# Copies out of PSUM ahead of sigmoid and weight splits on ScalarE in the dense stage, and a group's last preparation moved behind its output copies

## The chip, the cores and the metric

The kernel runs on one core of a Trainium2 chip. The metric is the device time of one execution in microseconds; lower is better. The engines are TensorE (PE in the profile, its weight loads PEld), VectorE (DVE), ScalarE (ACT), GpSimd (POOL) and SyncE (SP), which only issues transfers here. Each engine runs its own instructions in program order and waits for the others by semaphores.

## The reference, cut to what matters

An attention stage gives 4608 tokens of 512 numbers, a mixture of eight experts follows, and then the dense gated stage in which the change lies:

```python
def _moe2_ref(x, w_gate, w_val, w_out):      # x: 4608 x 512, 1536 hidden columns
    gate = 1.0 / (1.0 + np.exp(-(x @ w_gate)))
    val = x @ w_val
    return (gate * val @ w_out).astype(np.float32)
```

## The kernel before

The first two stages end near 714 us of the profiled execution; the function `ffn` does the dense stage. Every fp32 product is made of three matmuls on operands split into a high part (a rounded copy, made by ScalarE) and a low part (the rest, a subtraction on VectorE).

**Groups and steps.** `ffn` runs over groups `p`. Groups 0 to 3 are wide: 1024 tokens in two halves of 512, multiplied in a scheme of seven products in place of eight (`NK`, `ACTS`). Group 4 is narrow (`single`): 512 tokens in halves of 256. A group has twelve steps `j`, one for each 128 hidden columns. In a step PE makes products 0 to 6 with `prod` (L1417, six matmuls each): product 0 in `begin` of the step before, then `p1` to `p6`, into three kinds of PSUM banks: `ma` (products 0, 3, 4, 6), `mc` (1) and `md` (2, 5). `p5` adds into the `md` bank that `p2` wrote, after ScalarE's copy `v` (L1534) of the first sum; `p4` adds into the `ma` bank after ScalarE's copy `w` (L1539). `p1`'s bank is added to `u` on VectorE (L1523), and ScalarE takes a sigmoid of that (L1524); `p5` ends with an addition on VectorE (L1553) and a second sigmoid (L1554); `p4` with an addition to `v` (L1548); `p6` with the multiply of the gate (L1558), and GpSimd multiplies the other half's gate into `gB[j]` (L1564). Then `down` (L1453, twelve matmuls) adds the step before to the four output banks.

**Weights.** `fetch` reads a step's two weight tiles from memory (SP's queue, L863), `mix` makes sums and differences of them on GpSimd (L872 to L876), and `fill(j, i)` splits slot `i` (L883 on ScalarE, L884 on VectorE): slot 0 serves products 0 and 1, slot 1 products 2 and 3, slot 2 products 4 and 5, slot 3 product 6. `ready` fills slots 1 and 2 of the next step, calls `mix` for the step after it, and in group 0 also splits the output weight with `own(j, 1)`.

**Order.** The program order is written out by hand, and each engine keeps it. In steps 0 to 10 it is p1, p2, p3, p5, p4, `gated`, `ready`, `down(j - 1)`, `begin(j + 1)`, p6; in the last step p2, p3, p1, p4, p5, `gated`, p6, the split of the product, `ready`, `down(j - 1)`. The filling of slot 0 stands at the end of p1, that of slot 3 at the end of p3. After the last step the second half's twelve `down` products follow from `gB`, with transposes for the next group between them (`operands`). `fin` copies the four output banks (ScalarE and VectorE, L1464, L1466) and writes their rows with indirect transfers on GpSimd (L1467); each write waits until the one before has landed. At steps 1 and 2, `load` (L909) reads tokens for the next group, 1 MB each, on SP's queue behind the fetches of the step before.

Of the kernel before, what the change touches and what calls it, by code (L numbers as in the profile page):

```python
# [849 lines left out]
class Group:  # L850
# [60 lines left out]
    def gate(self, m):  # L911
        nc = self.nc
        t = self.tok[m] = self.sp.tile([P, 4], I32, tag="tok", name="tok")
        nc.gpsimd.tensor_copy(t, self.y[m][:, :, DM].bitcast(I32))
        g = self.gt[m] = self.sp.tile([P, 4], F32, tag="gt", name="gt")
        for r in range(4):
            nc.gpsimd.indirect_dma_start(
                out=g[:, r:r + 1], out_offset=None, in_=self.gd,
                in_offset=bass.IndirectOffsetOnAxis(ap=t[:, r:r + 1].bitcast(U32), axis=0))
# [462 lines left out]
def ffn(tc, ctx, c, grp, out):  # L1382
    nc = tc.nc
    V, A = nc.vector, nc.scalar
    NJ = DFF // P
# [9 lines left out]
    def own(j, part):  # L1395
        if part == 0:
            nc.sync.dma_start(out=w2[j][:, 1].bitcast(F32), in_=grp.wd[3 * j + 2])
        else:
            raw = w2[j][:, 1].bitcast(F32)
            A.activation(out=w2[j][:, 0], in_=raw, func=AF.Copy)  # L1400
            V.tensor_tensor(out=w2[j][:, 1], in0=raw, in1=w2[j][:, 0].bitcast(F32), op=ALU.subtract)
# [19 lines left out]
    def fetch(j, kind):  # L1421
        grp.fetch(j, kind, gp.tile([P, 512], F32, tag=("rg", "rv")[kind], name="rw", bufs=1 + kind))
# [3 lines left out]
    def mix(j, part):  # L1426
        if part == 0:
            s12s[j] = grp.dp.tile([P, 512], F32, tag="dsg", name="s12")
            grp.mix(j, s12s[j])
        else:  # L1430
            s34s[j] = gp.tile([P, 512], F32, tag="s34", name="s34", bufs=1)
            grp.mix(j, s12s[j], s34s[j])

    def fill(j, i):
        src = (lambda: grp.raws[j, 0], lambda: s12s[j], lambda: s34s[j], lambda: grp.raws[j, 1][:, 256:512])[i]()
        grp.fill(j, i, grp.slot(i), src)
# [19 lines left out]
    def sums():  # L1456
        return [ps_o.tile([P, DM], F32, tag="o", name="o") for _ in range(4)]

    def fin(m, o):
        tok = grp.tok.pop(m)  # L1460
        for r in range(4):
            t = op.tile([P, DM], F32, tag="os", name="os")
            if r % 2:
                A.activation(out=t, in_=o[r], func=AF.Copy)  # L1464
            else:
                V.tensor_copy(t, o[r])  # L1466
            d = nc.gpsimd.indirect_dma_start(  # L1467
                out=out, out_offset=bass.IndirectOffsetOnAxis(ap=tok[:, r:r + 1].bitcast(U32), axis=0),
                in_=t, in_offset=None)
            if m == NT // 4 - 1:  # L1470
                tc.declare_no_dep(d.ins, group="rows", reason="each token is in one place of the packed order")
                tc.add_to_no_dep_group("rows", d.ins)
# [4 lines left out]
    def begin(p, j):  # L1477
        a = bank("ma")
        prod(a, j, 0, True, False)
        u = gp.tile([P, 512], F32, tag="u", name="u")  # L1480
        A.activation(out=u[:, 0:grp.n], in_=a[:, 0:grp.n], func=AF.Copy)  # L1481
        banks[p, j] = a, u

    for p in range(NP + 1):
        single = p == NP
        n = 256 if single else 512
        if p == 0:
            fetch(1, 0)
            fetch(1, 1)
            mix(1, 0)  # L1490
            mix(1, 1)
            for j in range(NJ):
                own(j, 0)
            begin(p, 0)
        gB = []
        if not single:
            for tag in ("k3", "k4", "k5"):
                t = grp.kx.tile([P, 4, 512], F32, tag=tag, name="gb")
                gB += [t[:, i] for i in range(4)]
        o = sums()  # L1500
        g = None
        for j in range(NJ):
            end = j == NJ - 1
            one, two = (not single or j < NJ - k for k in (1, 2))
            n1, n2 = (j + 1) % NJ, (j + 2) % NJ
            a, sg = banks.pop((p, j))
            if j > 0:
                split(st["sg"], slice(0, 512), g)()
            if not single and p < NP:
                nxt = [2 * p + 2] + ([2 * p + 3] if p + 1 < NP else [])  # L1510
                for i, m in enumerate(nxt):
                    if j == 1 + i:
                        grp.load(m)
                    if j == 4 + i:
                        grp.gate(m)
                    if j == 7 + i:
                        grp.mult(m)
            now = {}

            def p1():  # L1520
                now["c"] = cb = bank("mc")
                prod(cb, j, 1, True, True)
                V.tensor_tensor(out=sg[:, 0:n], in0=sg[:, 0:n], in1=cb[:, 0:n], op=ALU.add)  # L1523
                A.activation(out=sg[:, 0:n], in_=sg[:, 0:n], func=AF.Sigmoid)  # L1524
                if one:
                    fill(n1, 0)
                if two:
                    fetch(n2, 0)

            def p2():  # L1530
                now["d"] = db = bank("md")
                prod(db, j, 2, True, False)
                now["v"] = t = gp.tile([P, 512], F32, tag="v", name="v", bufs=1)
                A.activation(out=t[:, 0:n], in_=db[:, 0:n], func=AF.Copy)  # L1534

            def p3():
                prod(a, j, 3, False, False)
                now["w"] = u = gp.tile([P, 512], F32, tag="w", name="w", bufs=1)
                A.activation(out=u[:, 0:n], in_=a[:, 0:n], func=AF.Copy)  # L1539
                if j > 0:  # L1540
                    fill(j, 3)
                if two:
                    fetch(n2, 1)

            def p4():
                t = now["v"]
                prod(a, j, 4, False, False)
                V.tensor_tensor(out=t[:, 0:n], in0=t[:, 0:n], in1=a[:, 0:n], op=ALU.add)  # L1548

            def p5():  # L1550
                db, u = now["d"], now["w"]
                prod(db, j, 5, False, True)
                V.tensor_tensor(out=u[:, 0:n], in0=u[:, 0:n], in1=db[:, 0:n], op=ALU.add)  # L1553
                A.activation(out=sg[:, n:] if single else u, in_=u[:, 0:n], func=AF.Sigmoid)  # L1554

            def p6():
                prod(a, j, 6, False, True)
                V.tensor_tensor(out=sg[:, 0:n], in0=sg[:, 0:n], in1=a[:, 0:n], op=ALU.mult)  # L1558

            def gated():  # L1560
                if single:
                    V.tensor_tensor(out=sg[:, n:], in0=sg[:, n:], in1=now["v"][:, 0:n], op=ALU.mult)
                else:
                    nc.gpsimd.tensor_tensor(out=gB[j], in0=now["w"], in1=now["v"], op=ALU.mult)  # L1564

            def ready():
                if p == 0:
                    own(j, 1)
                if one:
                    fill(n1, 1)  # L1570
                    fill(n1, 2)
                if two:
                    mix(n2, 0)
                    mix(n2, 1)

            for f in (p2, p3, p1, p4, p5) if end else (p1, p2, p3, p5, p4):
                f()
            gated()
            if end:
                p6()  # L1580
                last, g = g, pieces()
                split(sg, slice(0, 512), g)()
                ready()
                down(o, j - 1, last)
            else:
                ready()
                if j > 0:
                    down(o, j - 1, g)
                begin(p, j + 1)
                p6()  # L1590
                g = pieces()
            st["sg"] = sg
        if single:
            down(o, NJ - 1, g)
            return lambda: fin(2 * p, o)
        steps = grp.operands(p + 1, bank, small)
        h = pieces()
        split(gB[0], slice(0, 512), h)()
        next(steps)
        next(steps)  # L1600
        down(o, NJ - 1, g)
        fin(2 * p, o)
        fill(0, 3)
        o = sums()
        g = h
        for j in range(NJ):
            if j + 1 < NJ:
                h = pieces()
                split(gB[j + 1], slice(0, 512), h)()
            if j in (1, 2, 4, 5, 7, 8):  # L1610
                next(steps)
            down(o, j, g)
            g = h
        for _ in steps:
            pass
        begin(p + 1, 0)
        fin(2 * p + 1, o)
# [64 lines left out]
```

## Time and profile before

| | us |
|---|---|
| median of 3 runs | 1617.02 (1615.57 to 1620.66) |
| the profiled execution | 1617.71 |
| its span, first to last instruction | 1616.0 |
| PE busy | 1489.8 (92%) |
| PE waiting for the copy `v` (L1534) at `md` products | 38.7, in 51 waits |

A row of the timeline gives the start in us from the span's start, how long the row lasts, engine, line, operation, written tile <- read tiles, shape and count; in brackets the engine's idle time before it and what ended it. Neighbouring instructions of one kind are merged in one row (x6: six matmuls). Matmuls overlap, so the distance of two starts says more than a row's length.

### The profile page before, as it was taken

To read this page: it belongs to the slowest core of one execution; us is meant where nothing else is said; L and a number is where in the kernel's file an instruction comes from. 1 tells how busy PE (TensorE), PEld (TensorE's weight loads), DVE (VectorE), ACT (ScalarE), POOL (GpSimd) and SP (SyncE) were. 2 spreads that over 40 slices of the span, in tenths; PEclk is the share of its full clock that TensorE was granted. 3 is DMA by queue.
4 is the path that set the end of the run, shared out by engine and by line. 5 is a ranking of instruction groups with operands and counts; after the bars stand their busy time and mean duration, and the time that the engine had idled before them with its cause. 6 is when DMAs were issued, how large, how long until landed. Compare 5 with 4: busy or idle time off the path is not lost.

```text
span 1616.0 us, 22768 instructions
## 1 busy us (share of the span) xinstructions
PE 1489.8 (92%) x7314; PEld 1224.2 (76%) x7314; DVE 891.0 (55%) x1547; ACT 695.4 (43%) x1250; POOL 701.4 (43%) x688
## 2 busy tenths in 40 slices
PE   6889589999999998999999899999999999999887
PEld 3778468877888876877777777777777777778776
DVE  7788745444454544355556455565555645555554
ACT  3456444355333333354444434444344434443443
POOL 5554044344544556424663146532565234532322
PEclk7889889999999999999999999999999999999999
DMA  9874354475444463223111111112111121110211
GB/s 251 235 209 154 131 183 130 143 201 177 152 131 151 160 222 110 73 100 116 40 40 52 66 66 41 50 41 86 59 40 40 40 79 40 47 45 27 79 61 45
DMA packets 110407, 165.96 MB, mean 103 GB/s; under 512 B 23207, under 2 KB 68263, under 8 KB 108080
## 3 DMA queue, kind: packets, MB, share of 16 engines
q1 hardware_dynamic: 97904, 124.84, 25.6%
q0 software_dynamic: 10112, 28.88, 5.4%
q10 hardware_dynamic: 2240, 10.50, 1.8%
q8 instruction: 60, 0.98, 0.3%
q14 instruction: 91, 0.75, 0.1%
HBM read 126.41 MB, written 38.31 MB: 102 GB/s over the span
## 4 chain that ended last, share of the span: by engine, by line
PE 38%; ACT 6%; DVE 6%; issue 5%; DMA 2%; POOL 0%; POOLq 0%; ACTq 0%; DVEq 0%
PE o L1453 17%; PE ma L1417 14%; PE md L1417 6%; ACT wu L883 2%; ACT gh L1440 2%; DVE u L1523 2%; DVE u L1558 2%; DMA out<-os,tok 2%; ACT v L1534 1%; DVE wu L884 0%; PE b L942 0%; PE y L1084 0%; PE h L1084 0%; PE mc L1417 0%; PE a L942 0%
## 5 line engine op out<-in xcount | busy, mean ns | idle before, releaser
L1453 PE MATMUL o<-w,gh 128*128 128x512 f32 x864 | 270.2, 394 | 2.3 <-ACT os L1464 2.3
L1417 PE MATMUL md<-x,wu 128*128 128x512 f32 (+1 forms) x720 | 176.5, 381 | 38.7 <-ACT v L1534 38.7
L1453 PEld LDWEIGHTS o<-w,gh 128*128 128x128 f32 x864 | 160.7, 189 | 36.9 <-ACT os L1464 4.0
L1417 PEld LDWEIGHTS md<-x,wu 128*128 128x128 f32 x720 | 125.2, 191 | 79.0 <-ACT v L1534 58.4
L1564 POOL TENSOR_TENSOR gb<-w,v 128x512 f32<-128x512 f32 x48 | 75.0, 1563 | 242.2 <-DVE v L1548 179.8
L1417 PE MATMUL ma<-xT,wu 128*128 128x512 f32 (+1 forms) x720 | 170.0, 372 | 2.8 <-DVE v L1548 2.6
L1417 PE MATMUL ma<-x,wu 128*128 128x512 f32 (+1 forms) x720 | 167.5, 368 | 2.1 <-DVE x L948 2.1
L1453 PE MATMUL o<-w,gl 128*128 128x512 f32 x432 | 168.9, 391 | 0.0
L1417 PEld LDWEIGHTS ma<-xT,wu 128*128 128x128 f32 x720 | 128.2, 190 | 28.0 <-issue 4.2
L1417 PEld LDWEIGHTS ma<-x,wu 128*128 128x128 f32 x720 | 127.7, 188 | 25.6 <-DVE x L948 2.4
L884 DVE TENSOR_TENSOR wu<-rw,wu 128x256 fp32r<-128x256 f32 (+1 forms) x118 | 73.2, 621 | 107.8 <-ACT wu L883 107.8
L1084 PE MATMUL h<-h,xh 128*128 128x512 f32 x304 | 125.0, 411 | 7.6 <-ACT xh L1072 6.8
L884 DVE TENSOR_TENSOR wu<-s,wu 128x512 fp32r<-128x512 f32 x120 | 123.0, 1065 | 0.1
L1084 PE MATMUL h<-l,xh 128*128 128x512 f32 x304 | 121.8, 401 | 0.0
L1084 PE MATMUL h<-h,xl 128*128 128x512 f32 x304 | 121.8, 401 | 0.0
L1467 POOL DMA_INDIRECT out<-os,tok x36 | 37.4, 1039 | 187.8 <-DVE os L1466 107.4
L1481 ACT ACTIVATE u<-ma 128x512 f32<-128x512 f32 (+1 forms) x60 | 33.3, 556 | 169.3 <-PE ma L1417 165.9
L1558 DVE TENSOR_TENSOR u<-u,ma 128x512 f32<-128x512 f32 (+1 forms) x60 | 38.0, 634 | 119.0 <-PE ma L1417 119.0
L1148 POOL TENSOR_TENSOR dl<-dl,dsg 128x512 f32<-128x512 f32 x36 | 46.2, 1283 | 129.8 <-DVEq L1204 103.4
L1073 DVE TENSOR_TENSOR xl<-T,xh 128x512 fp32r<-128x512 f32 x38 | 26.3, 692 | 131.7 <-ACT xh L1072 130.5
L872 POOL TENSOR_TENSOR s<-rw 128x256 f32<-128x256 f32 x59 | 62.2, 1054 | 78.9 <-DMA rw<-wd 38.1
L1453 PEld LDWEIGHTS o<-w,gl 128*128 128x128 f32 x432 | 81.5, 189 | 17.4
(293 smaller groups left out, 3211.8 us busy)
## 6 DMA issues: line engine op xcount, KB each, us to landing
rw<-wd SPq DMA_DIRECT2D x118, 256.0 KB, 2.8
raw<-moe_w SPq DMA_DIRECT2D x46, 512.0 KB, 6.1
wd<-dw SPq DMA_DIRECT2D x36, 256.0 KB, 2.0
q<-q SPq DMA_DIRECT2D x8, 1024.0 KB, 6.6
k<-k SPq DMA_DIRECT2D x8, 1024.0 KB, 8.7
vb<-v SPq DMA_DIRECT2D x64, 128.0 KB, 4.8
xd<-xs ACTq DMA_DIRECT2D x8, 1024.0 KB, 4.5
draw<-moe_w_gate SPq DMA_DIRECT2D x12, 512.0 KB, 4.1
```

What stands on the lines that cost most here:

```text
L872: G.tensor_tensor(out=s12[:, lo], in0=v[:, lo], in1=v[:, hi], op=ALU.add)
L883: self.nc.scalar.activation(out=t[:, 0], in_=src, func=AF.Copy)
L884: self.nc.vector.tensor_tensor(out=t[:, 1], in0=src, in1=t[:, 0].bitcast(F32), op=ALU.subtract)
L1084: nc.tensor.matmul(ps, lhsT=a, rhs=b, start=(first and k == 0), stop=(last and k == n - 1))
L1148: G.tensor_tensor(out=lf, in0=lf, in1=s.bitcast(F32), op=ALU.mult)
L1417: nc.tensor.matmul(ps[:, 0:n], lhsT=w[:, a, cc * P:(cc + 1) * P], rhs=x[cc][:, b, 0:n], start=(first and i == 0), stop=(last and i == 5), ...
L1440: A.activation(out=gh[:, at], in_=src, func=AF.Copy)
L1453: nc.tensor.matmul(o[r], lhsT=a, rhs=b, start=(j == 0 and k == 0), stop=(j == NJ - 1 and k == 2))
L1467: d = nc.gpsimd.indirect_dma_start(out=out, out_offset=bass.IndirectOffsetOnAxis(ap=tok[:, r:r + 1].bitcast(U32), axis=0), in_=t, in_offse ...
L1481: A.activation(out=u[:, 0:grp.n], in_=a[:, 0:grp.n], func=AF.Copy)
L1558: V.tensor_tensor(out=sg[:, 0:n], in0=sg[:, 0:n], in1=a[:, 0:n], op=ALU.mult)
L1564: nc.gpsimd.tensor_tensor(out=gB[j], in0=now["w"], in1=now["v"], op=ALU.mult)
```

## The change

ScalarE's copies `v` and `w` keep their places behind p2 and p3. The sigmoid behind p1, with the filling of slot 0 and the first fetch, becomes a function `gate` that is called after p3 (in the last step after p4). The filling of slot 3 and the second fetch leave p3 and become `rest`, called after p4 (in the last step after p5, directly ahead of p6). In the last step `ready` is called after `fin(2 * p, o)` and not ahead of `down(j - 1)`; and `own(11, 1)` of group 0, which belonged to it, is made in step 10.

```diff
@@ p1
                 V.tensor_tensor(out=sg[:, 0:n], in0=sg[:, 0:n], in1=cb[:, 0:n], op=ALU.add)
+
+            def gate():
                 A.activation(out=sg[:, 0:n], in_=sg[:, 0:n], func=AF.Sigmoid)
                 if one:
                     fill(n1, 0)
@@ p3
                 A.activation(out=u[:, 0:n], in_=a[:, 0:n], func=AF.Copy)
+
+            def rest():
                 if j > 0:
                     fill(j, 3)
                 if two:
@@ ready
-                if p == 0:
+                if p == 0 and not end:
                     own(j, 1)
+                    if j == NJ - 2:
+                        own(j + 1, 1)
                 if one:
                     fill(n1, 1)
                     fill(n1, 2)
...
-            for f in (p2, p3, p1, p4, p5) if end else (p1, p2, p3, p5, p4):
+            for f in (p2, p3, p1, p4, gate, p5, rest) if end else (p1, p2, p3, gate, p5, p4, rest):
                 f()
             gated()
             if end:
                 p6()
                 last, g = g, pieces()
                 split(sg, slice(0, 512), g)()
-                ready()
                 down(o, j - 1, last)
...
         fin(2 * p, o)
+        ready()
         fill(0, 3)
```

## Rows read from the trace of the kernel before

**Rows 1.** The page: span, and busy time, share and instructions of each engine.

```profile
span 1616.0 us, 22768 instructions
PE 1489.8 (92%) x7314; PEld 1224.2 (76%) x7314; DVE 891.0 (55%) x1547; ACT 695.4 (43%) x1250; POOL 701.4 (43%) x688
```

**Rows 2.** PE's waits, groups 0 to 4 in turn: total us, times, longest us.

```profile
PE md L1417 <- ACT v L1534: 4.6, 10, 1.2
...
PE md L1417 <- ACT v L1534: 7.6, 10, 4.4
...
PE md L1417 <- ACT v L1534: 5.3, 10, 2.1
...
PE md L1417 <- ACT v L1534: 6.6, 10, 3.4
...
PE md L1417 <- ACT v L1534: 14.5, 11, 1.9
```

**Rows 3.** Timeline of PE, middle step of group 1: p2, p3, p5, p4.

```profile
940.63 1.52 PE L1417 MATMUL md<-x,wu 128*128 128x512 f32 x6
941.99 1.52 PE L1417 MATMUL ma<-x,wu 128*128 128x512 f32 x6
943.87 1.66 PE L1417 MATMUL md<-x,wu 128*128 128x512 f32 x6 [0.35 <-ACT v L1534]
945.37 1.52 PE L1417 MATMUL ma<-xT,wu 128*128 128x512 f32 x6
```

**Rows 4.** Timeline of ScalarE, same step: p1's sigmoid and the copy `v`.

```profile
942.18 0.63 ACT L1524 ACTIVATE u<-u 128x512 f32<-128x512 f32 x1 [1.36 <-DVE u L1523]
...
943.24 0.58 ACT L1534 ACTIVATE v<-md 128x512 f32<-128x512 f32 x1
```

**Rows 5.** Timeline of VectorE, same step: slots 1 and 2, then the multiply.

```profile
947.54 2.39 DVE L884 TENSOR_TENSOR wu<-s,wu 128x512 fp32r<-128x512 f32 x2
952.37 0.69 DVE L1558 TENSOR_TENSOR u<-u,ma 128x512 f32<-128x512 f32 x1 [2.43 <-PE ma L1417]
```

**Rows 6.** Timeline of PE, narrow group: p2, p3, p5 of step 10; p1, p4 of 11.

```profile
1588.83 0.88 PE L1417 MATMUL md<-x,wu 128*128 128x256 f32 x6
1589.55 0.88 PE L1417 MATMUL ma<-x,wu 128*128 128x256 f32 x6
1591.75 0.98 PE L1417 MATMUL md<-x,wu 128*128 128x256 f32 x6 [1.32 <-ACT v L1534]
...
1598.90 0.88 PE L1417 MATMUL mc<-x,wu 128*128 128x256 f32 x6
1599.88 0.98 PE L1417 MATMUL ma<-xT,wu 128*128 128x256 f32 x6
```

**Rows 7.** Timeline of group 1's last step: the copy for slot 3, p5, p6.

```profile
1058.84 0.41 ACT L883 ACTIVATE wu<-rw 128x256 fp32r<-128x256 f32 x1
...
1060.81 1.52 PE L1417 MATMUL md<-x,wu 128*128 128x512 f32 x6
...
1062.99 1.60 PE L1417 MATMUL ma<-xT,wu 128*128 128x512 f32 x6 [0.66 <-DVE v L1548]
```

**Rows 8.** Timeline of GpSimd and SP at group 1's start: output writes and a load.

```profile
915.42 0.96 POOL L1467 DMA_INDIRECT out<-os,tok  x1 [2.52 <-DMA out<-os,tok]
915.52 0.42 SPq L909 DMA_DIRECT2D yt<-yd  x1
...
925.67 0.96 POOL L1467 DMA_INDIRECT out<-os,tok  x1 [9.28 <-DMA out<-os,tok]
```

**Rows 9.** Stretches after two waits: length, busy us of engines, PEclk, DMA share, GB/s.

```profile
926.90:933.70 6.80, 5.09 (x12) 4.08 (x13) 1.69 (x2) 2.54 (x5) 3.99 (x5) 0.50 0.33 114
...
1317.00:1324.00 7.00, 3.58 (x16) 2.63 (x15) 2.39 (x4) 2.37 (x6) 5.74 (x6) 1.00 0.11 42
```

**Rows 10.** Timeline of SP and GpSimd, narrow group: fetches, and the first `mix` operation.

```profile
1582.86 0.87 SPq L863 DMA_DIRECT2D rw<-wd  x2
...
1586.20 0.73 POOL L872 TENSOR_TENSOR s<-rw 128x256 f32<-128x256 f32 x1 [6.29 <-DMA rw<-wd]
```

## The prediction, made before the changed kernel ran

> **What bounds the kernel now.** I read the page first: the span is 1616.0 us and nothing but TensorE is near full [rows 1]. The change touches the dense stage alone (`ffn`, from about 714 us on), so I then asked for the waits of PE in five stretches, one for each group: four wide ones (512 tokens twice, twelve steps each, then the second sum) and the narrow last one (256). In all five one wait leads, PE at an `md` product for ScalarE's copy `v` (L1534) [rows 2]. Then the timeline of one middle step, engine by engine, says why. PE issues p1, p2, p3 without a gap, each 1.36 us after the last, but p5 starts 1.88 us after p3 and p4 1.50 us after p5 [rows 3]. p5 adds into the bank that `v` is copied from, so it needs that copy. ScalarE is in order and has p1's sigmoid, at 942.18, and the copy of fill(n1,0) in front of it; `v` starts at 943.24 and ends at 943.82, PE starts at 943.87 [rows 3, 4]. p2's last matmul had ended at 942.15 (940.63 + 1.52). So the wait is one of queue order: `v` could have run a microsecond sooner. A middle step loses 0.52 + 0.14 = 0.66 us, of which the waits view shows 0.35; the other 0.31 is the restart. In the narrow group a product takes 0.72 us and p5 comes 2.20 us after p3: 1.48 lost, 1.32 of it in the view [rows 6].
>
> **Term A, p5 in the wide groups.** The change moves `v` and `w` in front of the sigmoid. `v` can start about 0.1 after p2's end, at 942.25, and end at 942.83; p5 could start at 943.35. Covered by 0.5. `w` starts after p3 (941.99 + 1.52 = 943.51), ends near 944.20, and p4 would start at 944.71: covered by 0.5 as well. What is moved behind: the sigmoid and fill(n1,0) now run near 944.2 to 945.4 instead of 942.2 to 943.3. Queued behind them are u's sigmoid, fill(j,3), fill(n1,1) and fill(n1,2), and on VectorE their subtractions. `begin` of the next step needs fill(n1,0) at about 948.8 (after p4 and twelve matmuls); the subtraction ends near 946, cover over 2 us. fill(j,3), behind u's sigmoid in the changed order, ends near 948.2; p6 needs it at about 950.2, cover 2 us. The last subtractions (2.39 us for two) ended at 949.93 and the next multiply on VectorE started at 952.37 [rows 5]; they move to about 950.6 and the multiply to 951.7, cover 1.1 us. Where a cover is gone, PE pays the excess in every step. On SP's queue fetch(n2,1) goes behind fill(j,3), some 3 us later, and GpSimd's mix with it; the result is wanted one step later. So the whole loss goes. From the four wide rows: 4.6 + 7.6 + 5.3 + 6.6 = 24.1 us in 40 waits [rows 2]; less the longest of the last three (4.4, 2.1, 3.4 = 9.9, term D), 14.2 in 37 waits, plus 37 x 0.31 of restarts: 25.7. Bounds: 25.7, or 19.8 if p4 has to wait 0.16 for `w` in each of 37 steps (the narrow group's last step shows such a wait: p4 starts at 1599.88 with `w` directly ahead of it, 0.98 after p1, which a row puts at 0.72 for a product [rows 6]; less 0.1 for the longer cover). I take 25.4.
>
> **Term B, the narrow group.** 14.5 in 11 waits, plus 11 x 0.16: 16.3 [rows 2, 6]. Here the covers are thin: `v` would end some 0.05 ahead of p5, and `w` likewise ahead of p4, since a product lasts 0.72 only. I leave 0.25 a step. In step 0 there is no down product to cover fill(1,0), which is now 2 us later, and the first steps also wait for mix(2) behind the output writes on GpSimd: 1.6 more. fetch(n2,1) is the other queue: the two fetches were issued from 1582.86 and mix started at 1586.20 [rows 10]; 2.5 us later still leaves mix a microsecond ahead of its reader. 16.3 - 2.7 - 1.6 = 12; bounds 9 and 16. PE idled for up to 1.9 here; if a fall of the clock as in [rows 9] goes with these waits, up to 3.4 more comes back, of which I add 0.9.
>
> **Term C, the end steps pay.** In a group's last step p6 follows p5 directly. Before, fill(j,3) was done early (1058.84, 0.41 us) and p6 waited for VectorE's add to `v` only: it started 2.18 after p5 instead of 1.36 [rows 7]. Now that add runs sooner, but fill(j,3) stands behind u's sigmoid, and that behind p5 itself. p5 ends at 1062.33; add u to about 1063.1, sigmoid (0.63 [rows 4]) to 1063.8, copy (0.41) to 1064.1: p6 near 1064.15 instead of 1062.99. The second half of the split is needed two matmuls later and just covered. So 1.2 us lost in each of four groups, and 1.5 by the same chain with narrow operations in the last: 6.3. Bounds 5 and 8 (all of the split needed at once, 0.4 more each). PE then idles for nearly 2 us; the granted clock stood at 0.50 (1.2 of 2.4 GHz) in 6.8 us behind the wait of 4.4, 3.4 lost, and at 1.00 behind the one of 3.4 [rows 2, 9]. So 0 to 3.4 for each; a shorter wait is nearer to the second row: I take 0.6, 2.5 in all.
>
> **Term D, the starts of groups 1 to 3.** Step 1's `v` there waits for GpSimd's multiply into gB[0], which stands behind four output writes, each waiting for the one before. The third was issued at 915.42, 2.52 us after the second was through; the 1 MB load of `yt` went out at 915.52, and the fourth write waited 9.28 us [rows 8]. The order of queues on GpSimd is unchanged, but SP's load stands behind fetch(2,0), which waits for fill(1,0); with the sigmoid 2 us later (944.1 for 942.18) the load goes out near 917.5, when the third write has a microsecond left. Then the fourth leaves near 918.9, gB[0] is done near 921, and `v`, wanted at 923, waits for nothing. Where an earlier write has slipped, the load hits the third anyway and the wait grows. The Trainium skill, DMA: Bandwidth & Descriptors, section "Issuing engines are not separate DMA queues", states that transfers of all issuing engines run on the same 16 DMA engines and interleave; the 9.28 us agrees, and by it the later load only chooses another victim, which could be the next write. Value: 9.9 + 3 x 0.31 = 10.8, and the 3.4 of slow clock: 14 if all three go, the upper bound; -6 if each grows by 2 us, the lower. I take 8, about two of three.
>
> **Term E, the rest.** `ready` behind `fin`: the fills of slots 1 and 2 were hidden and are now ahead of the splits of gB[1] on ScalarE and VectorE, where PE has 2.7 us of down products as cover; 0 to 0.8 a group, 0.3 taken, 1.2. mix(1) goes behind four writes on GpSimd and is wanted 30 us later: nothing. In group 0 `own(11, 1)` leaves the last step for step 10, where VectorE's cover takes it: at most half a microsecond either way, nothing taken. The stage's first sigmoid, with what has to be loaded for it, now stands behind the copies: 0.5 once, an estimate. Sum -1.7, bounds -5 and 0.
>
> **Sum.** 25.4 + 12.0 + 0.9 - 6.3 - 2.5 + 8.0 - 1.7 = 35.8 against the profiled execution (1617.71 us: the span and 1.71 around it) gives 1581.9; that run lies 0.7 above the median of 1617.02, so 1581.2. I say 1581.
>
> **Rivals.** (1) The group starts don't clear (D = 0 or worse, the load meets another write): 1589, up to 1595. For it: the writes slip by themselves now and then. (2) All three clear, no clock falls at the end steps, C at its small end: 1581 - 6 - 2.5 - 1 = 1571 or so. (3) The wait only changes place, against what the change says: p4 waits for `w` where p5 waited for `v`. A = 19.8 and B = 9: 1581 + 8.6 = 1590. Against it: the 0.5 us of cover in the wide steps. (4) Slower: VectorE becomes the bound. Its four two-operand subtractions of a step now lie beside GpSimd's multiply. Two of them took 1.19 each there, against 0.69 for the multiply of the same size [rows 5]. If each were held up by x more, a step would overrun its 1.1 us of cover by 4x - 1.1. Against it stand the 0.66 won and 0.28 that the other terms give per step (12.9 + 8.0 - 8.8 - 1.7 = 10.4 over 37 steps); the sign turns at x = 0.51. At 0.7: 37 x (1.7 - 0.94) = 28 slower, 1645. The Trainium skill, SBUF — State Buffer, section "Who interferes with whom", states that a VectorE instruction with two SBUF inputs and a reading GpSimd instruction exclude each other for a whole instruction. By that rule a hold could be as long as GpSimd's operation; the rows show half a microsecond, already in the 2.39, so the measurement speaks against it.
>
> **Chances.** Forecast 0.50 (1575 to 1587), rival 1 0.20, rival 2 0.14, rival 3 0.11, rival 4 0.05. The range for 8 in 10 takes in most of 1, 2 and 3: 1566 to 1597. A difference of 0.3% (4.9 us) is about what a measurement of this kernel can tell from none. Faster by more: all but rival 4 and a small part of 3, 0.93; within it 0.03; slower 0.04.
>
> **What would show it.** Right: in a middle step p5 starts 1.36 after p3, steps repeat every 12.24 us (54 matmuls of 1.36 / 6), and the waits of PE for `v` are gone from the wide groups; p6 of each last step starts near 3.3 after p5, waiting for the copy of fill(j,3); the fourth write of groups 1 and 3 comes 3.5 us after the third. Wrong: PE waits at p4 for `w`, at `begin` for `wu`, or ScalarE's gh waits for a late multiply on VectorE (covers gone); waits of 4 us and more at step 1 of groups 1 to 3 (D); slow clock in the slices behind each group's last step (C).

## The result, and the profile after

The changed kernel takes 1579.97 us (median of 4 runs, 1574.57 to 1581.91); the kernel before, run beside it, 1618.84. The ratio is 0.974, with a 95% interval of 0.968 to 0.980. The prediction said 1581, between 1566 and 1597. The page of the profiled execution (1579.18 us) answers to [rows 1]:

```profile
span 1577.4 us, 22746 instructions
PE 1468.6 (93%) x7314; PEld 1219.0 (77%) x7314; DVE 885.6 (56%) x1547; ACT 700.2 (44%) x1250; POOL 692.9 (44%) x688
```

The dense stage's first product starts at 714.01 us before and at 710.00 after. In ten profiled kernels whose code is the same up to there, that start lies anywhere from 710.0 to 721.5, so the 4 us are not the change's. I measure the stage itself, from that start to the end of the span: 902.0 us before, 867.4 after, 34.6 less.

**Where they went.** For each matmul of the stage I took the distance from its start to the next one's start, less what an undisturbed one needs (1.36 / 6 = 0.227 us, or 0.72 / 6 = 0.120 in the narrow group), and added up what is left by the product that came next. These sums leave 831.8 us in every kernel of this study, so they hold the whole difference. Losses in us, experiments included; labels are explained below:

| kernel | median | stage | p5 wide | p5 narrow | p4, p6 wide | p4, p6 narrow | at half clock | rest |
|---|---|---|---|---|---|---|---|---|
| before | 1617.0 | 902.0 | 35.9 | 17.3 | 4.1 | 0.5 | 7.2 | 5.1 |
| after | 1580.0 | 867.4 | 6.1 | 1.7 | 12.1 | 2.5 | 7.4 | 5.8 |
| e1_load_late | 1607.6 | 889.5 | 29.1 | 17.4 | 4.0 | 0.5 | 1.6 | 5.1 |
| e2_rest_back | 1563.6 | 846.7 | 3.6 | 1.7 | 0.3 | 0.8 | 3.0 | 5.5 |
| e3_ready_back | 1587.7 | 868.1 | 6.3 | 1.6 | 11.8 | 2.5 | 7.3 | 6.7 |
| e4_gb_behind | 1584.9 | 871.6 | 6.8 | 1.6 | 11.9 | 2.5 | 10.4 | 6.6 |
| e5_fill_only | 1589.1 | 875.2 | 14.8 | 13.9 | 4.0 | 1.1 | 4.5 | 5.1 |
| e6_w_behind | 1588.5 | 872.6 | 3.1 | 0.3 | 13.6 | 13.4 | 6.1 | 4.2 |
| e7_both | 1554.6 | 842.5 | 0.5 | 1.7 | 0.5 | 0.9 | 1.6 | 5.6 |
| e8_gb_vector | 1575.5 | 860.7 | 6.6 | 1.6 | 8.4 | 2.6 | 3.3 | 6.4 |

PE's waits of the changed kernel, for the stretches of groups 1, 2 and 4 (total us, times, longest), answer to [rows 2]:

```profile
PE ma L1417 <- ACT wu L883: 1.7, 1, 1.7
PE ma L1417 <- DVE wu L884: 0.6, 1, 0.6
...
PE md L1417 <- ACT v L1536: 6.0, 1, 6.0
PE ma L1417 <- ACT wu L883: 1.7, 1, 1.7
PE ma L1417 <- DVE wu L884: 0.6, 1, 0.6
...
PE ma L1417 <- ACT wu L883: 1.3, 1, 1.3
PE md L1417 <- ACT v L1536: 0.8, 2, 0.6
```

Ten or eleven waits a group for `v` became at most two. What is new is one pair in each wide group, for the two halves of a weight split (`wu`). The timeline of a middle step, PE (p3, p5, p4) and then ScalarE, answers to [rows 3, 4]:

```profile
950.39 1.52 PE L1417 MATMUL ma<-x,wu 128*128 128x512 f32 x6
951.75 1.52 PE L1417 MATMUL md<-x,wu 128*128 128x512 f32 x6
953.11 1.52 PE L1417 MATMUL ma<-xT,wu 128*128 128x512 f32 x6
...
950.65 0.60 ACT L1536 ACTIVATE v<-md 128x512 f32<-128x512 f32 x1 [1.43 <-PE md L1417]
952.01 0.60 ACT L1541 ACTIVATE w<-ma 128x512 f32<-128x512 f32 x1 [0.76 <-PE ma L1417]
952.50 0.62 ACT L1526 ACTIVATE u<-u 128x512 f32<-128x512 f32 x1
953.02 0.62 ACT L883 ACTIVATE wu<-rw 128x512 fp32r<-128x512 f32 x1
```

Products follow each other at 1.36 us. `v` starts 0.1 us after p2's end, and ends half a microsecond ahead of p5; the sigmoid and the fill come behind both copies.

### The profile page after: what moved, and what is told of

It is laid out like the page before. It is cut to its first block, busy times and chain, and to the rows that moved or that the text cites. A ratio compares the mean times of both kernels' runs of the same rounds, so it can differ in the third digit from the quotient of the medians.

```text
span 1577.4 us, 22746 instructions
## 1 busy us (share of the span) xinstructions
PE 1468.6 (93%) x7314; PEld 1219.0 (77%) x7314; DVE 885.6 (56%) x1547; ACT 700.2 (44%) x1250; POOL 692.9 (44%) x688
## 4 chain that ended last, share of the span: by engine, by line
PE 50%; DVE 2%; ACT 1%; DMA 1%; issue 1%; POOL 1%; POOLq 0%; DVEq 0%; ACTq 0%
PE o L1453 18%; PE ma L1417 18%; PE md L1417 9%; PE mc L1417 4%; DVE wu L884 1%; DMA out<-os,tok 1%; PE b L942 0%; PE a L942 0%; ACT wu L883 0%; PE y L1084 0%; PE h L1084 0%; DMA rw<-wd 0%; DVE w L1557 0%; POOL out L1467 0%; DVE x L948 0%
## 5 line engine op out<-in xcount | busy, mean ns | idle before, releaser
L884 DVE TENSOR_TENSOR wu<-rw,wu 128x256 fp32r<-128x256 f32 (+1 forms) x118 | 104.3, 884 | 178.4 <-ACT wu L883 178.4
L1417 PE MATMUL ma<-xT,wu 128*128 128x512 f32 (+1 forms) x720 | 172.0, 374 | 10.7 <-ACT wu L883 8.3
L1417 PE MATMUL md<-x,wu 128*128 128x512 f32 (+1 forms) x720 | 169.6, 371 | 6.8 <-ACT v L1536 6.7
L1568 POOL TENSOR_TENSOR gb<-w,v 128x512 f32<-128x512 f32 x48 | 64.7, 1348 | 139.2 <-ACT w L1558 129.9
L872 POOL TENSOR_TENSOR s<-rw 128x256 f32<-128x256 f32 x59 | 45.9, 778 | 145.8 <-DMA rw<-wd 131.9
L1100 ACT ACTIVATE hs<-h 128x512 f32<-128x512 f32 x76 | 45.3, 596 | 107.3 <-PE h L1084 105.1
L884 DVE TENSOR_TENSOR wu<-s,wu 128x512 fp32r<-128x512 f32 x120 | 85.2, 748 | 2.8 <-ACT wu L883 2.3
L1417 PE MATMUL mc<-x,wu 128*128 128x512 f32 (+1 forms) x360 | 84.8, 372 | 0.0
```

The lines of the kernel that those rows point to most:

```text
L872: G.tensor_tensor(out=s12[:, lo], in0=v[:, lo], in1=v[:, hi], op=ALU.add)
L884: self.nc.vector.tensor_tensor(out=t[:, 1], in0=src, in1=t[:, 0].bitcast(F32), op=ALU.subtract)
L1100: nc.scalar.activation(out=h, in_=st["hp", i][f], func=AF.Relu)
L1417: nc.tensor.matmul(ps[:, 0:n], lhsT=w[:, a, cc * P:(cc + 1) * P], rhs=x[cc][:, b, 0:n], start=(first and i == 0), stop=(last and i == 5), ...
```

## The experiments

**Theory.** Three terms make the gain and its price: the copies no longer stand behind a sigmoid and a fill (terms A and B), the fill of slot 3 comes too late for p6 in a group's last step (C), and the load of `yt` falls among output writes that wait for each other (D). **Rivals:** the sigmoid alone holds `v`, or the move of `w` is needed for nothing; `rest` has to go where it went; the writes slip whatever is loaded.

### Part of the move: the fill alone

```diff
 # the kernel before; the fill and the fetch behind v
-            for f in (p2, p3, p1, p4, p5) if end else (p1, p2, p3, p5, p4):
+            for f in (p2, p3, p1, gate, p4, p5) if end else (p1, p2, gate, p3, p5, p4):
```

Here `gate` holds only fill(n1,0) and fetch(n2,0); the sigmoid stays in p1.

> The kernel before, with a part of what `gate` moves: only fill(n1,0) and fetch(n2,0) go behind the copy `v`; the sigmoid stays ahead of it. Theory (everything queued on ScalarE ahead of `v` counts in proportion): `v` comes sooner by the length of the fill's copy, 0.4 us. A wide step loses 0.52 for it, so its loss falls from 0.66 to 0.1 or less: some 20 to 23 us less in 37 steps; a narrow step loses 1.48 and would still lose about 1.05: 5 us less in 11. Together 25 to 28 us less in the dense stage (902 us from its first product), with group starts that may move by 6 us either way: some 1591. Rival (the sigmoid, which waits for VectorE's add, is what holds `v`, and the copy of the fill only fills the gap behind it): the waits for `v` stay as they were, 24 and 14.5 us in the waits view, and the time is that of the kernel before.

Measured: 1589.1 us, ratio to before 0.978 (0.971 to 0.985). A middle step of the wide groups (p3, p5, p4 on PE's timeline):

```profile
952.60 1.52 PE L1417 MATMUL ma<-x,wu 128*128 128x512 f32 x6
953.95 1.65 PE L1417 MATMUL md<-x,wu 128*128 128x512 f32 x6
955.44 1.52 PE L1417 MATMUL ma<-xT,wu 128*128 128x512 f32 x6
```

and PE's waits in the narrow group:

```profile
PE md L1417 <- ACT v L1536: 11.2, 10, 1.4
```

A wide step loses 0.13 instead of 0.66, and p5's loss in all wide groups falls by 21.1; in the narrow group it falls by only 3.4 of 17.3. So in the wide steps the queue in front of `v` counts in proportion, and the fill's 0.5 us were about what a wide step was short of. The sigmoid is the rest, and matters in the narrow group. There the gain stayed under the forecast of 5: in steps 5 to 10 GpSimd's `mix` ran beside VectorE's subtraction for `gl` (L1441), which took 0.96 to 1.28 us where steps 1 to 4 show 0.69, and the sigmoid queued ahead of `v` came late with it.

### The second copy

```diff
 # the changed kernel
-(p1, p2, p3, gate, p5, p4, rest)
+(p1, p2, gate, p3, p5, p4, rest)
```

> The changed kernel with `gate` ahead of `w` again in every normal step, so that only `v` stands in front of the sigmoid. Theory: in a wide step `w` ends 0.7 later, about 0.2 ahead of p4, so nothing or some 0.1 us is lost there; in a narrow step a product lasts only 0.72 and p4 would wait for `w` by 0.6 to 0.8 in each of 11 steps: 7 to 9 us more than the changed kernel (867.4 us from the dense stage's first product), some 1588. It tells what the second of the two copies is worth. Rival (the prediction's rival 3, a cover of 0.5 in the wide steps that isn't there): p4 waits for `w` by 0.2 or more in some 40 wide steps as well, 17 us or more, 1597 and up. The other end: no wait at all, the move of `w` was not needed.

Measured: 1588.5 us, stage 872.6. The narrow group's waits name `w`:

```profile
PE ma L1417 <- ACT w L1541: 8.5, 10, 1.2
```

p4 and p6 lose 10.9 more than in the changed kernel in the narrow group (13.4 against 2.5); p5 gives 1.4 of that back and product 0 of step 1 another 0.6, so that the group loses 8.9 more in all, inside the forecast of 7 to 9. The wide groups lose 1.5 more at p4 and p6, nearly all in the first steps. Group 2's start was better here by chance (3.0 less at p5), which hides part of it in the total.

A middle step of the wide groups, `w` on ScalarE and then p4 on PE:

```profile
958.63 0.59 ACT L1541 ACTIVATE w<-ma 128x512 f32<-128x512 f32 x1
...
959.55 1.52 PE L1417 MATMUL ma<-xT,wu 128*128 128x512 f32 x6
```

`w` starts 0.28 after p3's end and not 0.1, so it is only 0.2 later than in the changed kernel (the forecast had 0.7), and still ends 0.3 ahead of p4. So `w` had to move only for the narrow group; there it is worth some 9 us.

### The last step: is `rest` needed behind p5?

```diff
 # the changed kernel: fill(j, 3) and fetch(n2, 1) again at the end of p3
-            def rest():
-                if j > 0:
+                if j > 0:
...
-(p2, p3, p1, p4, gate, p5, rest) ... (p1, p2, p3, gate, p5, p4, rest)
+(p2, p3, p1, p4, gate, p5) ... (p1, p2, p3, gate, p5, p4)
```

> The changed kernel with `rest` put back into `p3`: fill(j,3), the fetch and u's operations are done where the kernel before did them, and only the sigmoid and fill(n1,0) stay behind the copies. Theory: terms A and B come from `gate` alone, and `rest` behind p5 only brings term C. So in each wide end step p6 starts about 2.3 us after p5 and not 3.3, and loses 0.9 instead of 2.9 with the second wait; 4 x 2.0 + 1.7 of the narrow end step + 3.2 of half clock behind two of them = 12.9 less than the changed kernel: some 1567. Middle steps stay at 12.24 us with no wait for `v` or `w`. Rival: `rest` behind p5 is needed for the middle steps (with it ahead, the sigmoid and fill(n1,0) come behind fill(j,3) and `begin` or GpSimd's multiply waits): PE then shows waits for `wu` or `v` in the middle steps, 0.3 or more in each of some 40, and the time is that of the changed kernel or more, 1580 to 1592.

Measured: 1563.6 us, ratio to before 0.966 (0.959 to 0.973). In the changed kernel a wide group's last step looks like this (ScalarE, GpSimd, VectorE, then p6's six matmuls on PE; p5 started at 1038.79), to be held against [rows 7]:

```profile
1041.07 0.63 ACT L1558 ACTIVATE w<-w 128x512 f32<-128x512 f32 x1 [1.56 <-DVE w L1557]
1041.60 0.40 ACT L883 ACTIVATE wu<-rw 128x256 fp32r<-128x256 f32 x1
...
1041.77 1.27 POOL L1568 TENSOR_TENSOR gb<-w,v 128x512 f32<-128x512 f32 x1 [4.79 <-ACT w L1558]
...
1042.03 1.29 DVE L884 TENSOR_TENSOR wu<-rw,wu 128x256 fp32r<-128x256 f32 x1 [1.00 <-ACT wu L883]
...
1042.06 0.73 PE L1417 MATMUL ma<-xT,wu 128*128 128x512 f32 x2 [1.75 <-ACT wu L883]
1043.38 1.20 PE L1417 MATMUL ma<-xT,wu 128*128 128x512 f32 x4 [0.59 <-DVE wu L884]
```

With `rest` back (p5 and p6 on PE, then slot 3's copy and subtraction):

```profile
1038.52 1.52 PE L1417 MATMUL md<-x,wu 128*128 128x512 f32 x6
1039.88 1.52 PE L1417 MATMUL ma<-xT,wu 128*128 128x512 f32 x6
...
1036.55 0.41 ACT L883 ACTIVATE wu<-rw 128x256 fp32r<-128x256 f32 x1
...
1036.99 0.43 DVE L884 TENSOR_TENSOR wu<-rw,wu 128x256 fp32r<-128x256 f32 x1 [1.64 <-ACT wu L883]
```

p6 follows p5 at 1.36 with no loss at all, better than the 0.9 that I expected: with `v` copied early its addition is through in time, too. p4 and p6 lose 0.3 in the wide groups instead of 12.1, 0.8 in the narrow one instead of 2.5, no clock fall follows, and p5 keeps its whole gain. So A and B come from `gate` alone, and `rest` behind p5 cost some 16 us: 11.8 + 1.7 here and 3.0 of half clock behind two of the last steps. The stage is shorter by 20.7 in all; the other 4 lie in group 2's start and in a fall of the clock at the stage's entry that did not come, and neither is `rest`'s for certain.

### The second wait of p6

In the rows above VectorE's subtraction takes 1.29 us beside GpSimd's multiply, and 0.43 without it in the rows with `rest` back. The first try to tell the cause moved the multiply in the program order:

```diff
 # the changed kernel
+            if single or not end:
+                gated()
             if end:
                 p6()
+                if not single:
+                    gated()
```

> The changed kernel with one thing moved: in the last step of a wide group GpSimd's multiply into gB is issued behind p6's work instead of ahead of it. In the changed kernel VectorE's 128x256 subtraction of fill(j,3) takes 1.29 us beside that multiply, where it takes 0.43 alone, and p6 waits 0.6 to 0.76 a second time for it, at its third matmul. Theory A (the subtraction is held for the whole of GpSimd's operation, both reading SBUF): with the multiply elsewhere the subtraction takes 0.43 to 0.5 and the second wait of p6 goes, while the first, for the copy, stays: p6's loss falls from 2.9 to about 2.2 in four steps, and the time by 2 to 3 us, to some 1577. Theory B (it is held by something else, the issue or a late write of its input): it stays at 1.2 to 1.3 and the second wait stays.

Measured: 1584.9 us, ratio to before 0.977 (0.970 to 0.984). The subtraction of group 1's last step:

```profile
1045.23 1.29 DVE L884 TENSOR_TENSOR wu<-rw,wu 128x256 fp32r<-128x256 f32 x1 [1.00 <-ACT wu L883]
```

This settles nothing: p6 has no work for GpSimd, so the multiply is still next in GpSimd's queue, starts 0.26 ahead of the subtraction as before, and only its place in the text moved. The run is one more of the changed kernel, on the chip of e1 to e3. The second try takes the multiply away from GpSimd:

```diff
 # the changed kernel, in gated()
+                elif end:
+                    V.tensor_tensor(out=gB[j], in0=now["w"], in1=now["v"], op=ALU.mult)
```

> The changed kernel with the multiply into gB of a wide group's last step done by VectorE instead of GpSimd, in its place in VectorE's order behind the subtraction of fill(j,3). Nothing of GpSimd then runs beside that subtraction. Theory A (the subtraction, 1.29 us there, was held through GpSimd's whole multiply): it takes 0.43 to 0.5, and the second wait of p6, at its third matmul, goes: 0.6 to 0.8 us in each of four steps, 2.5 to 3.5 us in all, with the first wait of p6 (1.7, for the copy) unchanged. Theory B (its length has another cause): 1.2 to 1.3 again and the second wait stays. The clock falls behind these waits come and go between runs, 3.4 us each, so the two waits are what tells, not the time.

Measured: 1575.5 us, stage 860.7. VectorE and PE in group 1's last step (p5 started at 1038.63):

```profile
1041.88 0.43 DVE L884 TENSOR_TENSOR wu<-rw,wu 128x256 fp32r<-128x256 f32 x1 [1.00 <-ACT wu L883]
1042.22 0.68 DVE L1568 TENSOR_TENSOR gb<-w,v 128x512 f32<-128x512 f32 x1
...
1041.89 1.65 PE L1417 MATMUL ma<-xT,wu 128*128 128x512 f32 x6 [1.75 <-ACT wu L883]
```

The subtraction is back at 0.43, the second wait is gone, and p4 and p6 lose 8.4 instead of 12.1, 0.9 a step. The first wait is 1.75 to the digit. So the subtraction was held by GpSimd's operation: in the changed kernel's rows it ended 0.28 after that one's end (1043.32 and 1043.04).

### The load among the writes

```diff
 # the kernel before
-                    if j == 1 + i:
+                    if j == 2 + i:
                         grp.load(m)
```

> The kernel before, with one thing changed: the 1 MB load of the next group's `yt` is issued one step later (in step 2 of its group instead of step 1), when the four output writes of the group start are through. Theory of the prediction's term D (the load falls among writes that wait for each other, the fourth takes 9 us instead of 3.5, and with it gB[0] and step 1's `v` come late): the waits of PE for `v` of 4.4, 2.1 and 3.4 us in step 1 of groups 1 to 3 go, with 0.3 of restart each and up to 3.4 of half clock behind the first: 11 to 14 us less than the kernel before, some 1604. Rival (the writes slip by themselves, whatever is loaded): the waits stay within 2 us of what they were and the time is that of before, some 1617. A third outcome, that one group clears and another doesn't, would say that both are at work.

Measured: 1607.6 us, ratio to before 0.9935 (0.9897 to 0.9974). Third and fourth write of group 1, then the load:

```profile
917.49 0.96 POOL L1467 DMA_INDIRECT out<-os,tok  x1 [2.51 <-DMA out<-os,tok]
921.64 0.96 POOL L1467 DMA_INDIRECT out<-os,tok  x1 [3.19 <-ACT u L1481]
...
929.73 0.42 SPq L909 DMA_DIRECT2D yt<-yd  x1
```

The fourth write comes 4.2 us after the third instead of 10.3 [rows 8]. The longest waits for `v` in the groups' stretches are 0.5, 1.7 and 0.5 instead of 4.4, 2.1 and 3.4, and both clock falls behind them are gone. The stage is 12.5 shorter. Of that, 1.6 is a clock fall in the narrow group that failed to appear although the waits there are as long as before; 10.9 is the load's. The theory holds, just under its lower end of 11.

### `ready`

```diff
 # the changed kernel
                 split(sg, slice(0, 512), g)()
+                ready()
                 down(o, j - 1, last)
...
         fin(2 * p, o)
-        ready()
         fill(0, 3)
```

> The changed kernel with `ready` back where it was, ahead of the last step's `down` in every group, instead of behind `fin`. It tells term E's part for this edit (1.2 us lost in the prediction, nothing in the trace of the changed kernel). Theory from the trace: TensorE waits for neither order, so 0 within 1.5 us, some 1580. Rival: the old place costs what the change was made for, fills ahead of the output copies, so PE's waits for the copies `os` come back (1.28 instead of 0.61 in the first group, 0.35 instead of 0 in the fourth): 1 to 4 us more, up to 1584, or the group starts differ and the time moves by their 6 us waits either way.

Measured: 1587.7 us, ratio to before 0.982 (0.975 to 0.989); the stage of the profiled run takes 868.1, 0.7 more than with the change. Waits for the copies `os` are 0.5 at most, as after the change. On the same chip e4, which is the changed kernel in effect, took 1584.9; the ranges of the two overlap. So nothing that can be measured hangs on this edit. The move of `own(11, 1)` to step 10 stayed in this run; none takes it apart.

### The two best edits together

> The two edits that gained, together: the changed kernel with `rest` put back into `p3`, and the load of `yt` one step later. With `rest` put back the dense stage took 846.7 us from its first product; what it still lost was a wait of 3.4 us for `v` in step 1 of group 2 with 3.4 lost to half clock behind it. Theory (the load among the serial output writes makes that wait): both go, some 7 us less, 839 to 840, and a time near 1556. Rival (in group 2 the second write slips by 3 us by itself, in every run so far): a wait of 0.5 to 2 us stays there, with or without the fall of the clock: 841 to 845. Or the later load meets the next step's fetches, and another step waits for it: no gain, 847.

Measured: 1554.6 us, ratio to before 0.959 (0.951 to 0.966): 25 us below the changed kernel. PE's waits in the stretch of group 2 (one line is all there is), and the longest ones behind it, where the narrow group starts:

```profile
PE o L1453 <- ACT os L1464: 0.5, 1, 0.5
...
PE md L1417 <- ACT v L1536: 1.1, 2, 0.9
```

p5's loss in the wide groups is down to 0.5. The stage takes 842.5 rather than 839 to 840, mainly because a fall of the clock at the stage's entry (1.6, not there in the run with `rest` back alone) came back; no wait in step 1 of group 2 is left, as the theory had it. Of 10.7 us of losses little lies in the steps any more.

## Why the prediction was right, and where it was not

The forecast was a gain of 35.8 against the profiled execution; the stage gained 34.6. That the two lie so near is in part luck: B and E together came out 4.4 better than forecast, C and D 5.4 worse. And of the 38.5 us between the two profiled executions, 4.0 lie ahead of the stage. By its terms, from the table of losses and the waits behind it:

| term | forecast | measured | from |
|---|---|---|---|
| A, p5 wide | +25.4 | +25.1 | 35.9 - 10.8 for the group starts |
| B, narrow | +12.0, +0.9 clock | +14.5, +1.6 clock | 15.6, less 0.07 a step at p4 (0.6) and 0.5 in the rest |
| C, end steps | -6.3, -2.5 clock | -9.1, -3.0 clock | 7.7 wide (8.1 at p6, less 0.4 that p4 no longer loses), 1.4 narrow; 1.6 + 1.4 at half clock |
| D, group starts | +8.0 | +5.9 | waits 10.8 to 6.1, half clock 4.1 to 2.9 |
| E, rest | -1.7 | -0.5 | group 0, step 0 |

**A** was read off right, step by step: `v` 0.1 after p2, cover of half a microsecond at p5 and p4. In e6, with `w` 0.2 later, 0.3 of the second cover was left and p4 in the wide steps was still on time. Rival 3 (p4 waits for `w`) did not come; in the narrow group it would have, had `w` not been moved too.

**B** was mis-sized in the residual. I left 0.25 a step and 1.6 for the first steps because the covers were computed at 0.05; PE waits 0.6 at most, twice, and 0.07 in most steps. A thin cover in a computed schedule held. The clock's 1.6 is not the change's for certain: e1 has the same narrow waits and no fall.

**C** has the step that failed. Its first half came true: p6 3.27 after p5, waiting for the copy of fill(j,3), where I had said 3.3. "The second half of the split is needed two matmuls later and just covered" did not: the subtraction took 1.29 where I had counted on the 0.4 of the copy, and p6 waited again at its third matmul. A wide last step loses 2.9 us instead of 0.9, 2.0 each instead of 1.2.

The clock's part, 2.5 forecast and 3.0 measured, came near for a poor reason. That "a shorter wait is nearer to the second row", the one at full clock, does not hold in the trace of before: behind group 2's wait of 2.1 us [rows 2], the shortest of the three at the group starts, the granted clock was 0.50 too (columns as in [rows 9]):

```profile
1124.90:1128.30 3.40, 3.40 (x10) 2.63 (x9) 1.48 (x2) 0.64 (x3) 2.40 (x4) 0.50 0.00 0
```

Nor was "3.4 lost" behind the wait of 4.4 right: PE idled for part of those 6.8 us, and 2.5 were lost there.

The cause of C's second wait was in a row that I had read wrongly. The prediction took the 2.39 us for two subtractions [rows 5] as 1.19 each, half a microsecond of slowing per subtraction, and said that this speaks against a hold for a whole operation. The view of that line for the same stretch of the kernel before (min/median/max in ns):

```profile
L884 DVE TENSOR_TENSOR wu<-s,wu x2: 693/1238/1784, 947.5 to 948.2; 128x512 fp32r<-128x512 f32 x2
```

and GpSimd's timeline beside it:

```profile
947.75 1.63 POOL L1564 TENSOR_TENSOR gb<-w,v 128x512 f32<-128x512 f32 x1 [7.95 <-DVE v L1548]
```

One took 0.69 and was not slowed at all, although the multiply began 0.2 into it; the other, begun beside GpSimd's multiply, took 1.78 and ended 0.6 after the multiply's end at 949.38. It is one hold to the end of the other engine's operation, not a share: of the subtractions that began while this multiply was running, all 41 of the kernel before (128x512) ended 0.55 after it, and all 28 of size 128x256 in the changed kernel 0.28 after it. The Trainium skill, SBUF — State Buffer, section "Who interferes with whom", says just this of a VectorE instruction with two SBUF inputs and a reading GpSimd one; this trace and e8 agree with it, and the prediction should not have set it aside. Rival 4 still did not come: one hold per step stays one hold wherever it falls, and the middle steps have the cover for it.

**D** came out as described, in two of three groups. The writes and the load of groups 1 and 2 in the changed kernel, against [rows 8]:

```profile
906.47 0.96 POOL L1467 DMA_INDIRECT out<-os,tok  x1 [2.52 <-DMA out<-os,tok]
909.97 1.44 POOL L1467 DMA_INDIRECT out<-os,tok  x1 [2.54 <-ACT wu L883]
...
909.03 0.42 SPq L909 DMA_DIRECT2D yt<-yd  x1
...
1092.80 0.98 POOL L1467 DMA_INDIRECT out<-os,tok  x1 [5.58 <-ACT v L1536]
1096.31 0.97 POOL L1467 DMA_INDIRECT out<-os,tok  x1 [2.54 <-DVE v L1552]
1105.25 0.97 POOL L1467 DMA_INDIRECT out<-os,tok  x1 [7.97 <-DMA out<-os,tok]
...
1096.02 0.42 SPq L909 DMA_DIRECT2D yt<-yd  x1
```

In group 1 the later load goes out 2.56 after the third write and the fourth comes at 3.5, as forecast; PE has no wait there. But the load did choose another victim. The fourth write of group 1 takes 8.3 us from its issue to its landing:

```profile
L1467 POOL DMA_INDIRECT out<-os,tok x1: 1441/1441/1441, 910.0 to 910.0; - x1
...
DMA to landing us min/median/max: 8.3/8.3/8.3
```

That of group 3 takes 8.6; with the load 8.4 us after the fourth write (e7) they take 3.2 and 3.3, and the second and third writes there 2.7. No write follows the fourth, and GpSimd goes on to gB[0] without waiting for its landing, so the delay costs PE nothing. The prediction had drawn the case of the next write from the Trainium skill (DMA: Bandwidth & Descriptors, "Issuing engines are not separate DMA queues"), by which transfers of all issuing engines interleave; the trace agrees. In group 2 the second write had slipped by 2.8, the load went out 0.3 ahead of the third and met that one, and the wait for `v` grew from 2.1 to 6.0, the case that the prediction named ("where an earlier write has slipped"). "About two of three" was right; the price of the third was not in the 8.

## What to carry to other kernels

When an in-order engine holds up another, list everything queued between the awaited instruction and the moment its input is ready, and move just that: `gate` won all of it, while `rest`, moved as well, had stood in front of nothing that mattered and cost 16 us where a short step had no other work to cover it. A merged row hides which of its instructions is slow; before a mean is used as a price per instruction, look at the single ones. A transfer that can start at any time belongs behind a chain of transfers that wait for each other, not among them; here even the later load slowed one of them, and was harmless only where that was the last.

## What the runs showed of the hardware

**A dose for the collision.** A write of the chain lands 2.7 us after its issue where nothing disturbs it, and the next is issued 3.5 after it. How long after a write the load of `yt` goes out decides which write is slowed and by how much (us; e1 and e7, where the load comes behind all four, are left out):

| load issued after a write by | next write after it |
|---|---|
| 0.10, 0.11 (before, groups 1 and 3) | 10.3, 8.8 |
| 0.63, 0.63 (e5, groups 1 and 3) | 7.6, 8.1 |
| 0.82, 0.93 (group 2: before, e5) | 5.2, 5.4 |
| 1.16, 1.16, 1.53 (e6) | 5.0, 5.0, 5.4 |
| 2.05 (e2, groups 1 and 3) | 3.5, 3.5 |
| 2.56, 2.57 (after, e3, e4, e8: groups 1 and 3) | 3.5; this next write, the last, lands late (8.3 and 8.6 in the changed kernel) |
| 3.2 (group 2: after, e2, e3, e4, e8) | 3.5, but the one after that 6.9 to 9.7 later |

**A slip that stays open.** In group 2 the second write comes 6.1 to 7.1 us after the first in all ten kernels, and 3.8 in groups 1 and 3, with no load out yet. It is not the first write's transfer, which has landed after 2.7 to 3.6 in the six traces that show it. In all ten, one packet of the DMA queue that the profile calls q8, instruction, falls between these two writes, 0.5 to 4.2 us after the first, and none between the writes of groups 1 and 3. Whether it holds the second write is not shown; no experiment was made on it.

**The clock.** Behind the pair of waits in the last step (1.75 and 0.59 us) the granted clock falls to 0.50 (1.2 of 2.4 GHz) in some groups and not in others: in the changed kernel, e3 and e6 in groups 2 and 3, in e4 in all four. Two stretches of the changed kernel behind such a pair, groups 1 and 2 (columns as in [rows 9]):

```profile
1043.80:1047.20 3.40, 3.40 (x17) 2.74 (x16) 1.38 (x2) 0.66 (x2) 0.00 (x0) 1.00 0.22 77
1240.60:1244.00 3.40, 3.40 (x10) 2.63 (x9) 1.38 (x2) 0.63 (x1) 0.00 (x0) 0.50 0.28 81
```

In the four kernels with both waits it fell in 10 of 16 such steps; with the first wait alone (e8) in none of 4, and in none of 4 in the kernel before. Taking 0.59 us of idling away thus took the falls with it, some 3 us; four steps are few to call that a rule.
